# Two chained expert layers after sigmoid attention: block sums split where they are made, tokens loaded into free slots, stores on GpSimd's queue

## The chip, the cores and the metric

One core of a Trainium2 chip. The metric is the device time of one execution, in microseconds. A core has TensorE (PE; its weight loads are PEld), VectorE (DVE), ScalarE (ACT), GpSimd (POOL), SyncE (SP), and 16 DMA engines that serve all queues. Each engine runs its instructions in the order in which they were written.

## What is computed

```python
scores = scale * np.matmul(q, k.transpose(0, 1, 3, 2)) - np.log(S)   # q, k, v: 4 x 12 x 448 x 64
attn = 1.0 / (1.0 + np.exp(-scores))
x = np.matmul(attn, v)                         # then heads side by side: x is 1792 x 768
h = x @ w_in;  g = s * np.maximum(h, 0.0) ** 2 + b;  x = g @ w_out        # w_in 768 x 2048, w_out 2048 x 768
h = x @ w_in2; g = np.maximum(h, 0.0) + alpha * np.minimum(h, 0.0); out = g @ w_out2
```

All arrays are float32.

## The kernel before

**Arithmetic.** Each of the four large products is one step of a seven-product block scheme: the weights are cut in 2 x 2 blocks, sums of blocks (A11, A12, A22, S1 to S4) are made, and so are sums of token blocks; products M1 to M7 are formed in `IN_ORDER` or `OUT_ORDER` (lines 23 and 24) and added up on eviction. Each float32 operand is split in a rounded part (L322, ScalarE) and the rest (L325, VectorE), and each product is three matmuls, L406 to L408, of a 128 x 128 weight tile with 448 tokens.

**Stages.** First attention, in `NU` = 84 units (`qk`, `sig`, `av`, `take_x`). Then the tokens go through in two halves g = 0, 1, for each expert layer m = 0, 1: `phases` are (m, g) = (0,0), (0,1), (1,0), (1,1), and each has an in-phase (8 groups `mp` of seven products with the non-linear function after them) and an out-phase (seven products, three output blocks each). So eight half-phases of 504 matmuls follow attention.

**Weights.** The weights come in as 64-bit words. `quad` (L236) makes one block sum's worth: two loads into `R64`, `cva` on ScalarE (L263), L266 and L271 on VectorE, four additions (L284), and a store of 7 blocks to a DRAM tile (L302). There are 8 of kind "in" and 9 of kind "out" for each m, all made in the one buffer `QUAD`. `unit` (L309) loads 1024 columns of that DRAM tile into `RAW` and splits them into a `RING` entry, 21 units for every half-phase.

**Tokens.** `make_x` makes the seven token operands `X` out of four raw blocks `XRAW`, with VectorE subtractions (L335) and splits. For phases after the first, `load_x` loads the raw blocks from DRAM to `XRAW[1]`, which lies in `PROD`, over `R64`, `CVA` and a part of `QUAD`. It and `make_x` are written at the last product of the out-phase before (`middle[6]`).

**PSUM.** In an in-phase products M1 and M2 use one bank, M5 and M4 another, M6 and M7 a third: the second of each accumulates on the first, and must wait until the first was read (`pcopy` L417, `padd` L427).

**Order.** Everything but warm-up is added to a `Plan` with an engine, a cost and the cells that it reads and writes. `order` (L55) sets due times from TensorE's order and then, over and over, emits for the engine that can start first the operation that can start first, by those costs. The `"SP"` queue is one such engine, and carries all loads and all stores (L302, L526). Block sums are asked for by `produce`: 20 at attention unit 4, 9 after phase 0, the rest after phase 1.

Of the kernel before, what the change touches and what calls it, by code (L numbers as in the profile page):

```python
# [18 lines left out]
CELL = 64  # L19

IN_ORDER = ["M1", "M5", "M6", "M2", "M7", "M4", "M3"]
# [5 lines left out]
class Plan:  # L29
# [25 lines left out]
    def order(self):  # L55
# [5 lines left out]
        ideal, t = {}, 0.0  # L61
        for i, op in enumerate(self.ops):
            if op[0] == "PE":
                ideal[i] = t
                t += op[1]
        late = [0.0] * n
        for i in range(n - 1, -1, -1):
            eng, dur, lat = self.ops[i][:3]
            x = min((late[s] for s in succ[i]), default=t + 50) - dur - lat
            late[i] = min(x, ideal[i]) if i in ideal else x  # L70
        left = [len(op[3]) for op in self.ops]
        est = [0.0] * n
        pe = [i for i in range(n) if i in ideal]
# [5 lines left out]
        free = {}  # L79
        done = []  # L80
        while len(done) < n:
            best = None
            for eng, cand in open_.items():
                if not cand:
                    continue
                f = free.get(eng, 0.0)
                if eng == "PE":
# [13 lines left out]
            end = start + dur  # L101
            free[eng] = end
            done.append(i)
            for s in succ[i]:
                est[s] = max(est[s], end + lat)
# [3 lines left out]
        return done  # L109
# [26 lines left out]
def tile_kernel(  # L136
# [59 lines left out]
    RAW = [own(f"raw{i}", UNIT) for i in range(NRAW)]  # L196
    TMP = [own(f"tmp{i}", S) for i in range(NTMP)]
    NEG = own("neg", 2 * S)
# [7 lines left out]
    def act_t(n, psum=False):  # L206
        return (0.15 if psum else 0.19) + 0.834e-3 * n

    def dve_t(n, psum=False):
        return 0.155 + (1.06e-3 if psum else 1.04e-3) * n  # L210
# [4 lines left out]
    def dma_t(n):  # L215
        return 0.1 + n * 4 * P / 330e3
# [3 lines left out]
    MM = 0.2005  # L220
# [11 lines left out]

    w64 = {(0, "in"): w_in1, (0, "out"): w_out1, (1, "in"): w_in2, (1, "out"): w_out2}
    w32 = {k: drp.tile([P, 7 * NMP * WQ], F32, name=f"w{k[0]}{k[1]}") for k in w64}

    def quad(m, kind, k, c):  # L236

        order = IN_ORDER if kind == "in" else OUT_ORDER
# [8 lines left out]
        for row in range(2):  # L247
# [9 lines left out]
            x, y = ("A11", "A12") if row == 0 else ("S3", "A22")  # L257
# [18 lines left out]
            add("ACT", act_t(2 * n), f0, cv, ca)  # L276
# [11 lines left out]
        tt("S1", "S3", "A22", ALU.add)  # L288
        tt("S3", "A11", "S3", ALU.subtract)
# [7 lines left out]
        else:  # L297
# [4 lines left out]
            "SP", dma_t(7 * n), lambda: nc.sync.dma_start(out=dst, in_=src),  # L302
# [3 lines left out]
    n_unit = [0]  # L306
    ring = {}

    def unit(m, kind, i):  # L309
        g = n_unit[0]  # L310
        n_unit[0] += 1
        raw, dst = RAW[g % NRAW], RING[g % NRING]
        load(
            sb(raw, UNIT), w32[m, kind][:, i * UNIT : (i + 1) * UNIT], UNIT,
            [("d", m, kind, 8 * i + j) for j in range(8)], cells(raw, UNIT),
        )
        split(dst, dst + UNIT, raw, UNIT)
        ring[m, kind, i] = dst
# [27 lines left out]
    X = [[slots(f"xo{p}{i}", p, 3 * i, 3) for i in range(7)] for p in range(2)]  # L346
# [17 lines left out]
    def make_x(par, raw):  # L364
        p = [XRAW[raw] + i * XB for i in range(4)]
        pl = X[par]

        def half(i, src):
            split(pl[i], pl[i] + XB, src, XB)

        half(0, p[0])
        minus(p[0], p[1], p[0], XB)
        half(1, p[0])
        minus(p[0], p[3], p[0], XB)
        half(2, p[0])
        half(3, p[2])
        minus(p[1], p[3], p[1], XB)
        half(4, p[1])
        minus(p[0], p[0], p[2], XB)
        half(5, p[0])  # L380
        half(6, p[3])

    def load_x(m, g):
        for i in (0, 1, 3, 2):
            to = XRAW[1] + i * XB
            load(
                sb(to, XB), x_dram[m, g][:, i * XB : (i + 1) * XB], XB,
# [458 lines left out]
```

## Time and profile before

| | us |
|---|---|
| median of 3 runs | 1026.64 (1022.49 to 1033.18) |
| profiled execution | 1022.74 |
| its span, first to last instruction | 1020.9 |
| TensorE busy in the span | 972.0 (95%) |
| VectorE busy | 762.6 (75%) |
| ScalarE busy | 625.8 (61%) |
| GpSimd busy | 0.2 |
| moved by DMA | 222.7 MB, 218 GB/s on the mean |

A row of a group of instructions names line, engine, operation and tiles (out<-in). PEclk is the granted share of TensorE's clock. TensorE's busy time is that of pipelined matmuls, so a busy TensorE can still be waiting a little.

### The profile page before, as it was taken

What the parts mean: (1) busy time and instruction counts of PE and PEld (TensorE: products, weight loads), DVE (VectorE), ACT (ScalarE), POOL (GpSimd) and SP (SyncE); (2) the same over time, 40 slices, a digit from 0 to 9 for tenths busy, and PEclk for the clock granted to TensorE, in tenths of its full rate; (3) what the DMA queues carried; (4) which work ended last, traced back from release to release, by engine and by line L of the source; (5) the groups of instructions that cost most, each with busy time, mean ns of one, the idle gap of its engine ahead of it and who ended that gap; (6) DMA issues with size and microseconds to landing.
All of it is one profiled execution on the core that took longest, in us unless ns stands there. A gap on an engine that the chain in (4) does not pass through costs nothing.

```text
span 1020.9 us, 13856 instructions
## 1 busy us (share of the span) xinstructions
PE 972.0 (95%) x5424; PEld 828.7 (81%) x5424; DVE 762.6 (75%) x896; ACT 625.8 (61%) x675; POOL 0.2 (0%) x4
## 2 busy tenths in 40 slices
PE   9999999998699979999999889998999999999998
PEld 5533368987598968999899769997999999999997
DVE  2476467679996867668999589868997856679872
ACT  7889856877553536778665246656645455576440
POOL 0000000000000000000000000000000000000000
PEclk9999999998899999999999989998999999999999
DMA  8998999886776657776579568765444533333441
GB/s 302 332 336 300 354 330 353 281 286 193 275 258 223 208 185 285 239 253 222 166 241 313 198 233 281 226 216 200 116 122 147 163 111 111 104 106 105 146 138 67
DMA packets 70625, 222.68 MB, mean 218 GB/s; under 512 B 6688, under 2 KB 30624, under 8 KB 68512
## 3 DMA queue, kind: packets, MB, share of 16 engines
q1 hardware_dynamic: 70560, 221.81, 64.6%
q8 instruction: 42, 0.69, 0.3%
q14 instruction: 23, 0.19, 0.0%
HBM read 163.98 MB, written 57.80 MB: 217 GB/s over the span
## 4 chain that ended last, share of the span: by engine, by line
PE 62%; DVE 11%; DMA 6%; ACT 3%; issue 3%; SPq 0%; DVEq 0%; ACTq 0%
PE ps L406 21%; PE ps L408 21%; PE ps L407 21%; DMA xraw<-x 3%; DVE ring L325 2%; DVE xo L325 2%; DVE gb L325 1%; DVE g L335 1%; DVE quad L284 1%; DMA r<-in_w_in 1%; DVE xraw L335 1%; DVE tmp L427 1%; ACT gb L322 1%; DVE quad L271 1%; DMA raw<-w0in 1%
## 5 line engine op out<-in xcount | busy, mean ns | idle before, releaser
L406 PE MATMUL ps<-xo,ring 128*128 128x448 f32 x672 | 250.9, 373 | 22.3 <-DVE tmp L427 18.7
L322 ACT CAST ring<-raw 128x1024 fp32r<-128x1024 f32 x168 | 175.3, 1047 | 154.6 <-PE ps L407 111.9
L406 PE MATMUL ps<-gb,ring 128*128 128x448 f32 x672 | 249.1, 371 | 10.7 <-ACT ring L322 7.5
L408 PE MATMUL ps<-gb,ring 128*128 128x448 f32 x672 | 249.0, 371 | 9.4 <-DVE ring L325 9.4
L407 PE MATMUL ps<-xo,ring 128*128 128x448 f32 x672 | 249.0, 370 | 0.0
L408 PE MATMUL ps<-xo,ring 128*128 128x448 f32 x672 | 248.7, 370 | 0.0
L407 PE MATMUL ps<-gb,ring 128*128 128x448 f32 x672 | 248.1, 369 | 0.0
L325 DVE TENSOR_TENSOR ring<-raw,ring 128x1024 fp32r<-128x1024 f32 x168 | 204.2, 1217 | 24.7 <-ACT ring L322 24.6
L406 PEld LDWEIGHTS ps<-xo,ring 128*128 128x128 f32 x672 | 128.6, 191 | 39.3 <-DVE tmp L427 23.1
L406 PEld LDWEIGHTS ps<-gb,ring 128*128 128x128 f32 x672 | 128.2, 191 | 23.4 <-ACT ring L322 10.6
L408 PEld LDWEIGHTS ps<-gb,ring 128*128 128x128 f32 x672 | 128.0, 190 | 22.1 <-DVE ring L325 11.5
L408 PEld LDWEIGHTS ps<-xo,ring 128*128 128x128 f32 x672 | 128.5, 191 | 10.7
L407 PEld LDWEIGHTS ps<-xo,ring 128*128 128x128 f32 x672 | 128.5, 191 | 10.3
L407 PEld LDWEIGHTS ps<-gb,ring 128*128 128x128 f32 x672 | 128.3, 191 | 10.4
L427 DVE TENSOR_TENSOR tmp<-ps,tmp 128x448 f32<-128x448 f32 x124 | 76.7, 619 | 71.0 <-PE ps L408 58.2
L325 DVE TENSOR_TENSOR gb<-g,gb 128x1344 fp32r<-128x1344 f32 (+1 forms) x84 | 116.1, 1395 | 10.1 <-ACT gb L322 7.7
L322 ACT CAST gb<-g 128x1344 fp32r<-128x1344 f32 (+1 forms) x84 | 99.3, 1190 | 21.2 <-PE ps L408 14.5
L677 ACT ACTIVATE sg<-ps,bias 128x896 f32<-128x896 f32 x84 | 82.9, 1009 | 13.3 <-PE ps L661 12.6
L263 ACT ACTIVATE cva<-r 128x768 f32<-128x768 f32 (+1 forms) x68 | 59.0, 868 | 51.5 <-DVE quad L271 20.0
L271 DVE SCALAR_TENSOR_TENSOR quad<-cva,quad 128x768 uint32<-128x768 uint32 (+1 forms) x68 | 61.5, 905 | 30.6 <-DMA xraw<-x 18.5
L661 PE MATMUL ps<-kq 64*64 64x448 f32 x672 | 80.9, 542 | 2.0 <-ACT sg L677 2.0
L699 PE MATMUL ps<-sg,v 64*64 64x448 f32 x672 | 80.0, 536 | 0.0
(32 smaller groups left out, 656.8 us busy)
## 6 DMA issues: line engine op xcount, KB each, us to landing
r<-in_w_in SPq DMA_DIRECT2D x32, 768.0 KB, 5.4
raw<-w0in SPq DMA_DIRECT2D x42, 512.0 KB, 4.5
raw<-w0out SPq DMA_DIRECT2D x42, 512.0 KB, 4.3
raw<-w1in SPq DMA_DIRECT2D x42, 512.0 KB, 3.7
raw<-w1out SPq DMA_DIRECT2D x42, 512.0 KB, 3.5
r<-in_w_out SPq DMA_DIRECT2D x24, 768.0 KB, 5.9
w0in<-quad SPq DMA_DIRECT2D x8, 1344.0 KB, 7.5
w1in<-quad SPq DMA_DIRECT2D x8, 1344.0 KB, 5.3
```

Source lines behind the costliest of these rows:

```text
L263: nc.scalar.activation(a, hi, AF.Prelu, scale=2.0**-112, alpha=-(2.0**32))
L271: nc.vector.scalar_tensor_tensor(out=u, in0=a.bitcast(U32), scalar=3, in1=u, op0=ALU.logical_shift_left, op1=ALU.bitwise_or,)
L322: add("ACT", act_t(n), lambda: nc.scalar.copy(h, x), cells(src, n), cells(hi, n))
L325: lambda: nc.vector.tensor_tensor(out=l, in0=x, in1=h.bitcast(F32), op=ALU.subtract),
L335: lambda: nc.vector.tensor_tensor(out=o_, in0=x_, in1=y_, op=ALU.subtract),
L406: nc.tensor.matmul(d, wh_, ml_, start=first and k == 0, stop=False, **opt)
L407: nc.tensor.matmul(d, wh_, mh_, start=False, stop=False, **opt)
L408: nc.tensor.matmul(d, wl_, mh_, start=False, stop=last and k == n, **opt)
L427: lambda: nc.vector.tensor_tensor(out=d, in0=bank(k), in1=o, op=ALU.add),
L661: nc.tensor.matmul(ps[h * D : (h + 1) * D, k + j, :S], a.ap[rows, S + k0 : S + k0 + D], a.ap[rows, :S], start=True, stop=True,)
L677: lambda: nc.scalar.activation(o, i, AF.Sigmoid, bias=sb(BIAS, 1), scale=QKSCALE),
L699: nc.tensor.matmul(ps[j * D : (j + 1) * D, k + h, :S], va[keys, v : v + D], a.ap[keys, j * S : (j + 1) * S], start=first, stop=last,)
```

## The change

Block sums for the first in-phase are kept in on-chip memory and split from there (`direct`), with a second buffer (`quadb`) over the place of `RAW` and `NEG`; they are still stored for the second half. Two in-sums and seven out-sums are asked for in attention, the other six in-sums and two out-sums inside the first in-phase, and all of m = 1 after that phase. Raw tokens (`XRAW[1]`) lie in five slots between the others, and in `NEG`. `IN_ORDER` has M4 before M7. All stores are issued by GpSimd. The plan is placed three times, each time with TensorE's start times of the time before as goals; loads and stores share one modelled pipe there, and some costs are changed. `MORE` is empty, so nothing is saved in split form.

```diff
-IN_ORDER = ["M1", "M5", "M6", "M2", "M7", "M4", "M3"]
+QUEUES = {"SP": 0.07, "POOL": 1.0}
+AHEAD = 1.0
+ROUNDS = 3
+EARLY = 7
+MORE = []
+IN_ORDER = ["M1", "M5", "M6", "M2", "M4", "M7", "M3"]
...
+        for _ in range(ROUNDS):
+            late = [0.0] * n
+            for i in range(n - 1, -1, -1):
+                dur, lat = self.ops[i][1:3]
+                x = min((late[s] for s in succ[i]), default=t + 50) - dur - lat
+                late[i] = min(x, goal[i]) if i in goal else x
+            done, at = self.place(succ, late, list(goal))
+            goal = {i: at[i] for i in goal}
+        return done
...
                 f = free.get(eng, 0.0)
+                if eng in QUEUES:
+                    f = max(f, pipe - AHEAD)
...
-            end = start + dur
-            free[eng] = end
+            if eng in QUEUES:
+                free[eng] = start + QUEUES[eng]
+                pipe = max(pipe, start) + dur
+                end = pipe
+            else:
+                end = free[eng] = start + dur
...
-    XRAW = {0: tensor("xraw0", RING0, 4 * XB), 1: tensor("xraw1", PROD, 4 * XB)}
+    SPARE = take(NRAW * UNIT + 2 * S)
+    RING4 = [tensor(f"rinq{i}", RING0 + i * 4 * WQ, 4 * WQ, F32R) for i in range(4)]
+    RAW = [tensor(f"raw{i}", SPARE + i * UNIT, UNIT) for i in range(NRAW)]
+    NEG = tensor("neg", SPARE + NRAW * UNIT, 2 * S)
+    MID = SLOTS + 16 * SLOT
+    XRAW[1] = [
+        [(tensor("xraw10", MID + 2 * SLOT, XB), 0, XB)],
+        [(tensor("xraw11", MID, XB), 0, XB)],
+        [(tensor("xraw12", MID + 2 * SLOT + XB, XB), 0, XB)],
+        [(tensor("xraw13", MID + XB, S), 0, S), (tensor("xraw14", NEG.base, 2 * S), S, XB)],
+    ]
-    QUAD = tensor("quad", PROD + 10 * WQ, 7 * WQ)
+    QUADS = [tensor("quad", PROD + 10 * WQ, 7 * WQ), tensor("quadb", SPARE, 7 * WQ)]
...
-    MM = 0.2005
+    MM = 0.2035
...
-        tt("S1", "S3", "A22", ALU.add)
-        tt("S3", "A11", "S3", ALU.subtract)
+        tt("S3", "A11", "S1", ALU.subtract)
+        tt("S1", "S1", "A22", ALU.add)
...
-            "SP", dma_t(7 * n), lambda: nc.sync.dma_start(out=dst, in_=src),
+            "POOL", dma_t(7 * n), lambda: nc.gpsimd.dma_start(out=dst, in_=src),
...
+    def direct(mp, place):
+        for b0, b1 in ((0, 2), (2, 4), (4, 6), (6, 7)):
+            n = (b1 - b0) * WQ
+            dst = entry((7 * mp + b0) * WQ, n, RING4)
+            split(dst, dst + n, QUADS[place] + b0 * WQ, n)
+            yield
...
-    X = [[slots(f"xo{p}{i}", p, 3 * i, 3) for i in range(7)] for p in range(2)]
+    X = [
+        [slots(f"xo{p}{i}", 0, k, 3) for i, k in enumerate(ks)]
+        for p, ks in enumerate(([0, 3, 6, 9, 12, 18, 15], [34, 31, 28, 25, 22, 19, 16]))
+    ]
...
+            if m == g == 0:
+                get = direct(mp, 1 - mp % 2)
             for i, x in enumerate(IN_ORDER):
...
+                    if m == g == 0 and i % 2 == 0 and kc == 0:
+                        next(get)
...
+            if m == 0 and g == 0 and mp + 2 < NMP:
+                if mp % 2 == 1 and EARLY + mp // 2 < len(outs):
+                    quad(*outs[EARLY + mp // 2])
+                quad(m, "in", mp + 2, 0, 1 - mp % 2)
...
-        add("SP", dma_t(S), lambda: nc.sync.dma_start(out=d, in_=x), cells(src, S), w, DMA_LAT)
+        add("POOL", dma_t(S), lambda: nc.gpsimd.dma_start(out=d, in_=x), cells(src, S), w, DMA_LAT)
...
-    for m in range(2):
-        quads += [(m, "in", k, 0) for k in range(NMP)]
-        quads += [(m, "out", k, c) for c in range(len(CHUNKS)) for k in range(NDP)]
+    quads = [(0, "in", 0, 0, 1)]
+    outs = [(0, "out", k, c) for c in range(len(CHUNKS)) for k in range(NDP)]
+    quads += outs[:EARLY]
+    quads += [(0, "in", 1, 0, 0)]
+    quads += [(1, "in", k, 0) for k in range(NMP)]
+    quads += [(1, "out", k, c) for c in range(len(CHUNKS)) for k in range(NDP)]
...
-            produce(20)
+            produce(2 + EARLY)
...
+        if n == 0:
+            produce(len(quads))
         middle = {}
...
-        if n == 0:
-            produce(9)
-        if n == 1:
-            produce(len(quads))
```

## Rows read from the trace of the kernel before

**Rows 1.** Busy time by stretch (start:end, length; xinstructions; PEclk, DMA share, GB/s).

```profile
0.00:134.00 134.00, 130.96 (x1392) 61.24 (x1392) 71.09 (x101) 115.02 (x134) 0.20 (x4) 1.00 0.90 323
134.00:248.00 114.00, 105.72 (x508) 95.53 (x504) 85.60 (x125) 80.95 (x82) 0.00 (x0) 0.98 0.86 296
248.00:369.40 121.40, 110.17 (x505) 98.56 (x506) 102.66 (x110) 61.35 (x66) 0.00 (x0) 0.93 0.67 226
369.40:481.70 112.30, 104.75 (x505) 95.61 (x504) 79.06 (x107) 77.71 (x75) 0.00 (x0) 0.98 0.74 254
481.70:591.70 110.00, 104.51 (x505) 95.71 (x505) 95.00 (x102) 59.25 (x63) 0.00 (x0) 0.98 0.69 227
591.70:710.20 118.50, 108.87 (x506) 98.46 (x505) 97.81 (x129) 70.02 (x84) 0.00 (x0) 0.94 0.70 236
710.20:812.40 102.20, 102.20 (x506) 94.64 (x506) 90.30 (x80) 56.89 (x57) 0.00 (x0) 1.00 0.43 131
812.40:915.10 102.70, 102.50 (x505) 94.50 (x504) 66.07 (x77) 58.21 (x69) 0.00 (x0) 1.00 0.36 108
915.10:1017.40 102.30, 102.30 (x505) 94.50 (x504) 74.35 (x69) 46.35 (x48) 0.00 (x0) 1.00 0.38 118
```

The five busy times in a row are PE, PEld, DVE, ACT and POOL.

**Rows 2.** Waits of PE: who for whom, us in total, times, longest.

```profile
PE ps L406 <- DVE tmp L427: 20.0, 10, 5.0
PE ps L408 <- DVE ring L325: 9.4, 5, 3.6
```

**Rows 3.** Chain that ended last, 310 to 345 us: start, us, what.

```profile
311.76 5.35 DMA xraw<-x
...
326.84 5.14 DMA w1in<-quad
...
332.00 3.87 DMA xraw<-x
```

**Rows 4.** Tile `quad`: ns min/median/max, first to last start; then idle causes.

```profile
L302 SPq DMA_DIRECT2D w0out<-quad x9: 525/525/604, 148.4 to 262.0; - x9
...
L302 SPq DMA_DIRECT2D w0in<-quad x8: 326/326/424, 27.4 to 132.4; - x8
...
  DMA xraw<-x: 24.8, 6
```

**Rows 5.** DMA issues: count, KB each, median us to landing.

```profile
raw<-w0in SPq DMA_DIRECT2D x42, 512.0 KB, 4.5
...
w0in<-quad SPq DMA_DIRECT2D x8, 1344.0 KB, 7.5
w1in<-quad SPq DMA_DIRECT2D x8, 1344.0 KB, 5.3
...
out_yt<-tmp SPq DMA_DIRECT2D x24, 224.0 KB, 1.9
...
sc<-in_s SPq DMA_DIRECT2D x1, 0.5 KB, 6.5
```

**Rows 6.** Groups of instructions by form: busy, mean ns, idle before.

```profile
L325 DVE TENSOR_TENSOR ring<-raw,ring 128x1024 fp32r<-128x1024 f32 x168 | 204.2, 1217 | 24.7 <-ACT ring L322 24.6
...
L427 DVE TENSOR_TENSOR tmp<-ps,tmp 128x448 f32<-128x448 f32 x124 | 76.7, 619 | 71.0 <-PE ps L408 58.2 <-ACT tmp L417 10.4 <-PE ps L661 1.8
...
L284 DVE TENSOR_TENSOR quad<-quad 128x384 f32<-128x384 f32 x112 | 57.7, 551 | 5.8 <-DMA xraw<-x 4.0 <-ACT xo L322 0.9
L271 DVE SCALAR_TENSOR_TENSOR quad<-cva,quad 128x768 uint32<-128x768 uint32 x56 | 53.3, 952 | 24.6 <-DMA xraw<-x 14.5 <-ACT cva L263 10.1
...
L266 DVE TENSOR_SCALAR quad<-r 128x768 uint32<-128x768 uint32 x56 | 29.1, 554 | 25.0 <-DMA w0in<-quad 14.5 <-DMA w0out<-quad 5.2 <-DMA r<-in_w_in 5.2
```

**Rows 7.** Busy time by stretch, one of 25 us in the third out-phase.

```profile
725.00:750.00 25.00, 25.00 (x125) 23.16 (x125) 25.00 (x22) 12.11 (x13) 0.00 (x0) 1.00 0.44 129
```

**Rows 8.** Waits of SyncE's queue: who for whom, us in total, times, longest.

```profile
SPq L229 <- DVE ring L325: 450.5, 150, 7.9
SPq L302 <- DVE quad L284: 55.3, 26, 4.3
```

More of the change, by code (lines that the diff above doesn't have):

```diff
@@ L60, in order, with place @@
                 succ[d].append(i)
-        ideal, t = {}, 0.0
+        goal, t = {}, 0.0
         for i, op in enumerate(self.ops):
             if op[0] == "PE":
-                ideal[i] = t
+                goal[i] = t
                 t += op[1]
[L66 to L70, printed above, removed]
+        for _ in range(ROUNDS):
[7 more added lines that the diff above has]
+        return done
+    def place(self, succ, late, pe):
+        n = len(self.ops)
         left = [len(op[3]) for op in self.ops]
         est = [0.0] * n
-        pe = [i for i in range(n) if i in ideal]
         pe_at = 0
@@ L78, in order @@
                 open_.setdefault(self.ops[i][0], set()).add(i)
-        free = {}
-        done = []
+        free, done, at = {}, [], {}
+        pipe = 0.0
         while len(done) < n:
@@ L301, in quad, with saved, entry, unit @@
         add(
-            "SP", dma_t(7 * n), lambda: nc.sync.dma_start(out=dst, in_=src),
+            "POOL", dma_t(7 * n), lambda: nc.gpsimd.dma_start(out=dst, in_=src),
             cells(QUAD, 7 * n), wrote, DMA_LAT,
         )
-    n_unit = [0]
+    whl = {k: drp.tile([P, 2 * 7 * NMP * WQ], F32R, name=f"s{k[0]}{k[1]}") for k in SAVED}
+    n_unit = [0, 0]
     ring = {}
-    def unit(m, kind, i):
-        g = n_unit[0]
+    def saved(m, kind, at, n):
+        return whl[m, kind][:, 2 * at : 2 * (at + n)], [("h", m, kind, at)]
+    def entry(at, n, ring_=RING):
+        dst = ring_[n_unit[0] % len(ring_)]
         n_unit[0] += 1
-        raw, dst = RAW[g % NRAW], RING[g % NRING]
+        for j in range(n // P):
+            ring[at // P + j] = (dst + j * P, dst + (n + j * P))
+        return dst
+    def unit(m, kind, i, g):
+        at, n = i * UNIT, UNIT
+        dst = entry(at, n)
+        if (m, kind) in SAVED and g == 1:
+            src, there = saved(m, kind, at, n)
+            load(sb(dst, 2 * n), src, 2 * n, there, cells(dst, 2 * n))
+            return
+        raw = RAW[n_unit[1] % NRAW]
+        n_unit[1] += 1
         load(
-            sb(raw, UNIT), w32[m, kind][:, i * UNIT : (i + 1) * UNIT], UNIT,
-            [("d", m, kind, 8 * i + j) for j in range(8)], cells(raw, UNIT),
-        )
-        split(dst, dst + UNIT, raw, UNIT)
-        ring[m, kind, i] = dst
+            sb(raw, n), w32[m, kind][:, at : at + n], n,
+            [("d", m, kind, 8 * i + j) for j in range(8)], cells(raw, n),
+        )
+        split(dst, dst + n, raw, n)
+        save(m, kind, at, n, dst)
+    def save(m, kind, at, n, dst):
+        if (m, kind) in SAVED:
+            d, there = saved(m, kind, at, n)
+            x = sb(dst, 2 * n)
+            add(
+                "SP", dma_t(2 * n), lambda: nc.sync.dma_start(out=d, in_=x),
+                cells(dst, 2 * n), there, DMA_LAT,
+            )
+    def direct(mp, place):
[4 more added lines that the diff above has]
+            yield
     def split(hi, lo, src, n):
@@ L364, in make_x, with less @@
     def make_x(par, raw):
-        p = [XRAW[raw] + i * XB for i in range(4)]
-        pl = X[par]
+        p, pl = XRAW[raw], X[par]
         def half(i, src):
-            split(pl[i], pl[i] + XB, src, XB)
+            for t, a, e in src:
+                split(pl[i] + a, pl[i] + (XB + a), t, e - a)
+        def less(o, x, y):
+            for t, a, e in x if len(x) > 1 else y:
+                n = e - a
+                o_, x_, y_ = (z[0][0] + a if len(z) == 1 else t for z in (o, x, y))
+                minus(o_, x_, y_, n)
         half(0, p[0])
-        minus(p[0], p[1], p[0], XB)
+        less(p[0], p[1], p[0])
         half(1, p[0])
-        minus(p[0], p[3], p[0], XB)
+        less(p[0], p[3], p[0])
         half(2, p[0])
         half(3, p[2])
[L377 to L380, printed above, removed]
+        less(p[0], p[0], p[2])
+        half(4, p[0])
+        less(p[1], p[3], p[1])
+        half(5, p[1])
         half(6, p[3])
@@ L704, in f @@
                 )
[L706 removed]
+        add("PE", 0.80, f, r + w, w, PE_LAT)
     def take_x(q):
@@ L712, in take_x @@
         o = (2 * kh + bb % 2) * XB + i * S
-        t = XRAW[0] + o if bb < 2 else tmp()
+        t = XRAW[0][2 * kh + bb][0][0] + i * S if bb < 2 else tmp()
         pcopy(t, k)
```

64 lines of the change are left out of this document (31 added, 33 removed).

## The prediction

> **What bounds the kernel now.** I read the time by stretches first, cut where TensorE changes its work [rows 1]: attention (0 to 134 us), then four in-phases and four out-phases of 504 matmuls each. The last three take 102.2, 102.7 and 102.3 us, and TensorE is busy for all but 0.2 us of them: that is the floor of a half-phase, TensorE-bound at a granted clock of 1.00. The five before them take 114.0, 121.4, 112.3, 110.0 and 118.5 us, 576.2 together, which is 64 us above five floors of 102.45 (the mean of the 102.2 and the 102.7). The clock in those five rows is 0.93 to 0.98, so part of the excess is matmuls run slower after a stall. Attention has DMA busy 0.90 of the time at 323 GB/s and ScalarE busy 115 of 134 us.
>
> What ends TensorE's waits [rows 2]: the first matmul of a group waits for `tmp` from L427 (20.0 us, 10 times), that is a VectorE eviction of a PSUM bank that the next product accumulates in; and half of a ring entry comes late from L325 (9.4 us). These rows name the last link. The chain of waits names the cause behind it. At 310 to 336 us [rows 3], the end of the first out-phase, it alternates between the tokens' loads (`xraw<-x`, 5.35 and 3.87 us among them) and a block sum's store (`w1in<-quad`, 5.14 us): XRAW[1] lies in PROD, over R64, CVA and QUAD, so the next tokens land where a block sum is still being made, and each waits for the other. VectorE's block-sum instructions alone sat idle 24.8 us for `xraw<-x` [rows 4]. The first out-phase's beginning has another cause: 17 block sums of `m` = 0 are made one after another in one buffer, at (132.4 - 27.4)/7 = 15.0 and then (262.0 - 148.4)/8 = 14.2 us each [rows 4], so the last store leaves at 262.0 us, 14 us into the phase that reads it.
>
> **The change, part by part.** *Attention.* Nine block sums are asked for instead of a free run of 20; before, eight were stored by 132.4 us [rows 4]. Loads, stores and ScalarE's 115 us stay about as they are, TensorE's rate too. I take 0, from -3 (fewer ScalarE instructions between sigmoids) to +3.
>
> *First in-phase.* 21 of the 42 `raw<-w0in` loads of 512 KB go [rows 5], 11 MB. The splits now read QUADS directly, so block sum mp+2 is made while product group mp runs. VectorE decides. One group of seven products costs it 2688 columns of splits at 1.217 us per 1024 (3.2 us, some 3.4 in four instructions), five PSUM additions at 0.619 (3.1), and, for one block sum, 2 x 0.554 + 2 x 0.952 + 4 x 0.551 = 5.2 us [rows 6]: 11.7 us, in a group of 102.45/8 = 12.8. Eight groups of splits and additions are 52 us, six and a half block sums 34, the two out-sums left over (one is two thirds wide) 9: 95 us. The highest share that VectorE has in a phase at the floor is 90.3 of 102.2, 0.884 [rows 1]; 95/0.884 = 107.5. So the phase lies between 102.45 and 107.5 if nothing else stalls, and above that if a sum comes late. I take 108, against 114: -6. The order M2, M4, M7 helps here: M7, which accumulates in M6's bank, came two products after M6 and now comes three, M4 after M5 three instead of four. One product is three terms of three matmuls, 12.7/7 = 1.8 us, which is about the mean wait on L427 (20.0/10 = 2.0 us [rows 2]).
>
> *First out-phase to third in-phase.* XRAW[1] moves into five slots that are free in an out-phase, and NEG; the tokens' loads then wait for no block sum, and no sum for them. All 17 sums of `m` = 0 are finished by then, and the 17 of `m` = 1 have the stretch to about 650 us. At 14.2 us each [rows 4] they need 241 us of the 412 there are, so their pace is no bound. VectorE's work is unchanged: 102.7 + 79.1 + 95.0 + 97.8 = 374.5 us [rows 1]. At the floor these four phases take 409.8; if VectorE can't go above 0.884, 374.5/0.884 = 423.7. I take 419, two thirds of the way, since it does reach 25.0 of 25 us with TensorE at 25.0 in some stretches [rows 7]. Before: 121.4 + 112.3 + 110.0 + 118.5 = 462.2. So -43.
>
> *The last three phases* are at their floor: 0.
>
> *Stores on GpSimd's queue.* SyncE's queue stood 55.3 us before stores until their sums were done [rows 8], with loads behind. That queue is freed, but what mostly holds the loads is their own buffer (450.5 us for `ring`), so I count nothing for it. GpSimd does nothing in this trace but four memsets, and no row shows what a DMA from its queue costs. Call the delay of a store's landing L. Its bounds: below, -1 us or so, a store that no longer waits behind loads; above, 6.5 us, what even 0.5 KB took to land in a full queue [rows 5]. I take 1 us: the nearest row is the smallest store on an idle queue, `out_yt<-tmp`, 1.9 us of which 224 KB at 323 GB/s are 0.7, so 1.2 fixed, and a second such fixed part is the guess. Where L hurts: seven sums of attention stand in line for QUADS[0], so (0, "in", 1) comes 7L later. By the pace of 15.0 us (the first, in the other buffer, out at 27.4, the second 8 later) the seventh leaves near 35 + 6 x 15 = 125, lands near 132 and the in-sum is ready near 139; its splits start near 134 + 12.8 - 2 = 144.6. That is 5 us of slack. Two more out-sums stand before in-sums 3 and 5, with 1 and 3 us of slack. The price is 9L - 9 us: 0 at L = 1. The end gets 1 us longer by L (the last store ends the span).
>
> *A rule against it.* L266 takes 554 ns for 768 columns, L271 952 [rows 6], so L266 runs at about double rate and the other sum instructions don't. The Trainium skill (SBUF — State Buffer, Summary: rules for kernel authors) says of just such instructions that they lock GpSimd out while it writes a DMA's descriptors, and advises SyncE's or ScalarE's queue instead. By that rule a store waits for up to one L266, L grows by 0.55, and the sum by 5 us. No row here shows it, since GpSimd issues nothing.
>
> **Sum.** The profiled execution took 1022.74 us (span 1020.9). 1022.74 - 6 - 43 + 1 = 974.7, say 975. It lies 0.4% under the median of 1026.64, so the forecast stands a little low against that.
>
> **Rivals.** *Stores land late on GpSimd's queue (L = 3).* For: the seven stores in line are the only long serial chain that the change makes. Against: 15 us of pace has slack in it. 9 x 3 - 9 = 18: 993.
>
> *VectorE becomes the bound.* It needs 374.5 of 409.8 us. Where it was mixed with sums it reached 95.0 of 110.0 and 97.8 of 118.5, 0.84 on the mean [rows 1]; 374.5/0.84 = 446, 27 more than I count: 1002. Against: 24.8 us of its idle time is waits of the sums for `xraw<-x` [rows 4], which go.
>
> *The handovers stay.* What holds them could be the splits of the tokens (11 instructions of 1344 columns on VectorE, by the 1.217 us for 1024 [rows 6] an estimated 1.6 each, 17 us) and not their loads; then out-to-in handovers keep their excess in the second and third in-phases, 112.3 + 118.5 - 2 x 102.45 = 26, and some 9 of the out-phases before: 1010. Against: the fourth handover does the same splits with the tokens loaded before, and its phase is at the floor [rows 1].
>
> *Slower.* One mechanism: the line of stores through QUADS[0] in attention and the first in-phase, with GpSimd's landing so late that TensorE starves in the first in-phase. It decides from 9L - 9 = 48, L = 6.3 us, a landing of 12 to 14 us where 5.3 to 7.5 were [rows 5]. At L = 8: 63 us, 1038. For: the out-sums' stores are cut in seven rows per partition, and GpSimd's price is unknown. Against: even 6.5 us took a full queue.
>
> **How the numbers follow.** Forecast 975 (its own range 960 to 988): 0.56. Late stores 993: 0.16. VectorE 1002: 0.12. Handovers stay 1010: 0.08. Slower 1038: 0.08. A change of 1% is about what can be told from none here (three runs lie 1022.5 to 1033.2). Faster by over 1% (below 1016): the first three and a quarter of the fourth, 0.86; within 1%: the rest of the fourth, 0.06; slower 0.08. The range runs from 958 (attention 3 us shorter, phases near 410 and 103) to 1005; the last two cases lie above it, and some of the first three at its ends.
>
> **What would show it.** First out-phase to third in-phase each 103 to 107 us with clock 0.98 or more; no `xraw<-x` in the chain; waits on `tmp` L427 under 6 us; no store of `w0out` after 200 us; first in-phase near 108. Wrong, if the wait before the first in-phase's ring splits is for a store or a block sum (late stores), if VectorE is above 0.9 of those phases and TensorE still waits for L325, or if GpSimd's issues show several us each.

## The result and the profile after

The changed kernel takes 996.5 us (median of 4 runs, 992.3 to 1004.0) against 1024.9 for the kernel before: 0.9717 of it, 95% interval 0.9635 to 0.9799. The forecast was 975 with a range of 958 to 1005. The time lies in the range, and the gain is 28 us where 48 were summed. The profiled execution took 992.3 us, its span is 990.1.

Busy time of the changed kernel by stretch, cut where TensorE changes its work, with the columns of [rows 1] (PE, PEld, DVE, ACT, POOL; then PEclk, DMA share, GB/s); the last row is the end after the last matmul:

```profile
0.00:138.30 138.30, 133.15 (x1393) 61.24 (x1393) 73.03 (x104) 115.55 (x138) 13.26 (x23) 1.00 0.89 318
138.30:241.80 103.50, 102.39 (x508) 94.55 (x504) 93.16 (x147) 78.66 (x87) 6.13 (x10) 1.00 0.74 267
241.80:346.40 104.60, 102.80 (x505) 94.61 (x506) 96.71 (x94) 66.20 (x69) 7.32 (x13) 1.00 0.61 205
346.40:448.50 102.10, 102.10 (x505) 94.62 (x504) 77.46 (x103) 75.70 (x74) 3.22 (x6) 1.00 0.75 260
448.50:550.70 102.20, 102.20 (x506) 94.69 (x506) 95.78 (x93) 62.13 (x64) 6.50 (x12) 1.00 0.56 187
550.70:652.90 102.20, 102.20 (x506) 94.48 (x504) 91.31 (x127) 65.34 (x78) 6.82 (x8) 1.00 0.84 291
652.90:778.00 125.10, 108.36 (x506) 97.44 (x506) 105.11 (x104) 63.26 (x66) 7.76 (x13) 0.93 0.49 158
778.00:880.10 102.10, 102.10 (x505) 94.65 (x504) 66.05 (x78) 57.73 (x69) 0.54 (x1) 1.00 0.37 110
880.10:984.50 104.40, 104.23 (x505) 94.36 (x504) 75.41 (x70) 46.31 (x48) 5.96 (x11) 1.00 0.37 115
984.50:990.10 5.60, 0.00 (x0) 0.00 (x0) 0.62 (x1) 0.00 (x0) 0.54 (x1) 0.86 0.10 41
```

| us | before | by the prediction's sum | after |
|---|---|---|---|
| attention | 134.0 | 134.0 | 138.3 |
| first in-phase | 114.0 | 108 | 103.5 |
| first out-phase to third in-phase | 462.2 | 419 | 411.1 |
| third out-phase | 102.2 | 102.2 | 125.1 |
| last two phases | 205.0 | 205.0 | 206.5 |
| end | 3.5 | 4.5 | 5.6 |
| span | 1020.9 | 972.7 | 990.1 |

What was to be gained was gained, 12 us more than summed in the first five phases. But a phase that was at its floor before has a new stall of 23 us. TensorE's waits (who for whom, us in total, times, longest), to be read beside [rows 2]:

```profile
PE ps L480 <- ACT ring L386: 11.0, 3, 6.1
PE ps L480 <- DVE gb L389: 4.7, 3, 2.7
PE ps L482 <- DVE ring L389: 4.0, 4, 1.7
```

TensorE's waits on `tmp` are gone from the half-phases, and waits on a ring's split (11.0 and 4.0 us) hold most of what is left. Behind the longest of them, on the chain that ended last between 640 and 690 us (start, us, what), and then in the timeline of SyncE, ScalarE and TensorE (start, us; in brackets the engine's idle time before and what ended it):

```profile
659.42 5.59 DMA w1out<-quad
```

```profile
665.06 6.45 SPq L257 DMA_DIRECT2D raw<-w1out  x2
...
668.45 1.04 ACT L386 CAST ring<-raw 128x1024 fp32r<-128x1024 f32 x1 [1.44 <-DMA raw<-w1out]
...
669.55 0.74 PE L480 MATMUL ps<-gb,ring 128*128 128x448 f32 x1 [6.09 <-ACT ring L386]
```

TensorE waits for a weight whose block sum is stored only now: the load leaves as the store lands (659.42 + 5.59 = 665.01), the split follows the load, and the matmul the split. This store leaves 6.5 us into the phase that reads it, the last one 17 us. Not all of the 23 us is standing: TensorE's busy time in that phase is 108.4 instead of 102.2, so some 6 us are matmuls that ran slower. After TensorE had stood, the granted clock was about 0.5, the lower of its two levels (1.2 of 2.4 GHz):

```profile
665.00:675.00 10.00, 4.90 (x13) 3.94 (x14) 9.79 (x14) 4.22 (x6) 0.89 (x1) 0.52 0.51 157
```

The stores of the sums, by name (tile `quad`: ns min/median/max, first to last start), beside [rows 4]:

```profile
L332 POOL DMA_DIRECT2D w0out<-quad x9: 891/902/939, 35.0 to 187.5; - x9
L332 POOL DMA_DIRECT2D w1out<-quad x9: 891/895/912, 557.9 to 670.3; - x9
L332 POOL DMA_DIRECT2D w1in<-quad x8: 533/539/539, 297.0 to 541.2; - x8
```

The out-sums of m = 0 now end at 187.5 us, 54 us before the phase that reads them (before: 262.0, 14 us inside it). The eight in-sums of m = 1 take from 297 to 541 us, far more than eight times 14 us. The nine out-sums leave from 557.9 to 670.3, one each 14.1 us, and the last two of them in the third out-phase.

### The profile page after: what moved, and what is told of

The parts are those of the page before. It is cut to its first block, busy times and chain, and to the rows that moved or that the text cites. A ratio compares the mean times of both kernels' runs of the same rounds, so it can differ in the third digit from the quotient of the medians.

```text
span 990.1 us, 13931 instructions
## 1 busy us (share of the span) xinstructions
PE 959.5 (97%) x5424; PEld 820.7 (83%) x5424; DVE 774.6 (78%) x916; ACT 630.9 (64%) x689; POOL 58.1 (6%) x98
## 4 chain that ended last, share of the span: by engine, by line
PE 49%; issue 41%; DMA 3%; DVE 2%; POOL 2%; ACT 2%; POOLq 0%; SPq 0%; ACTq 0%; DVEq 0%
PE ps L482 13%; PE ps L480 13%; PE ps L481 13%; PE ps L740 5%; PE ps L778 4%; DMA r<-in_w_out 1%; DMA r<-in_w_in 1%; ACT sg L756 1%; POOL x L606 1%; POOL w1out L332 1%; POOL out_yt L606 1%; DMA w1out<-quad 1%; DVE ring L389 0%; ACT cva L293 0%; DVE g L399 0%
## 5 line engine op out<-in xcount | busy, mean ns | idle before, releaser
L386 ACT CAST ring<-raw 128x1024 fp32r<-128x1024 f32 x147 | 153.8, 1047 | 142.4 <-PE ps L481 123.9
L389 DVE TENSOR_TENSOR ring<-raw,ring 128x1024 fp32r<-128x1024 f32 x147 | 179.3, 1220 | 27.1 <-ACT ring L386 26.7
L480 PE MATMUL ps<-xo,ring 128*128 128x448 f32 x504 | 184.1, 365 | 0.0
L481 PE MATMUL ps<-xo,ring 128*128 128x448 f32 x504 | 184.1, 365 | 0.0
L482 PE MATMUL ps<-xo,ring 128*128 128x448 f32 x504 | 184.1, 365 | 0.0
L481 PEld LDWEIGHTS ps<-gb,ring 128*128 128x128 f32 x672 | 127.4, 190 | 10.5
L480 PEld LDWEIGHTS ps<-xo,ring 128*128 128x128 f32 x504 | 94.7, 188 | 7.5
L482 PEld LDWEIGHTS ps<-xo,ring 128*128 128x128 f32 x504 | 94.7, 188 | 7.5
L481 PEld LDWEIGHTS ps<-xo,ring 128*128 128x128 f32 x504 | 94.7, 188 | 7.5
L740 PE MATMUL ps<-kq 64*64 64x448 f32 x672 | 86.7, 545 | 2.9 <-ACT sg L756 2.7
L778 PE MATMUL ps<-sg,v 64*64 64x448 f32 x672 | 86.6, 536 | 1.2 <-DVE tmp L501 1.2
L399 DVE TENSOR_TENSOR g<-g 128x1344 f32<-128x1344 f32 (+1 forms) x48 | 66.3, 1396 | 2.3 <-ACT xo L386 2.2
```

The costliest lines, as they stand in the source:

```text
L386: add("ACT", act_t(n), lambda: nc.scalar.copy(h, x), cells(src, n), cells(hi, n))
L389: lambda: nc.vector.tensor_tensor(out=l, in0=x, in1=h.bitcast(F32), op=ALU.subtract),
L399: lambda: nc.vector.tensor_tensor(out=o_, in0=x_, in1=y_, op=ALU.subtract),
L480: nc.tensor.matmul(d, wh_, ml_, start=first and k == 0, stop=False, **opt)
L481: nc.tensor.matmul(d, wh_, mh_, start=False, stop=False, **opt)
L482: nc.tensor.matmul(d, wl_, mh_, start=False, stop=last and k == n, **opt)
```

## The experiments

### Is the new stall the late sums, and what makes them late?

Three theories. A: VectorE has no more time for the sums. B: stores from GpSimd land later, and that stretches the cycle of each sum. C: the plan's due times. It is placed three times, and each time takes TensorE's delayed starts as the new goals, so a late sum no longer counts as late.

**The sums of the second out-weight left out.**

```diff
-            sb(raw, n), w32[m, kind][:, at : at + n], n,
-            [("d", m, kind, 8 * i + j) for j in range(8)], cells(raw, n),
+            sb(raw, n), w32[0 if kind == "out" else m, kind][:, at : at + n], n,
+            [("d", 0 if kind == "out" else m, kind, 8 * i + j) for j in range(8)], cells(raw, n),
...
-    quads += [(1, "out", k, c) for c in range(len(CHUNKS)) for k in range(NDP)]
```

> The changed kernel without the nine out-sums of m = 1: the last two out-phases read the out-sums of m = 0 instead, so the second layer's second weight is left out. Theory A or any theory in which these sums are the cause of the new stall: third out-phase from 125.1 to 102 to 104 us, everything before the third in-phase unchanged to 1 us, profiled time about 992.3 - 22 = 970, which is close to the 975 that was forecast. A rival, that the stall comes from the tokens' loads into the middle slots and NEG (xraw loads at 651 to 674 us, with landings of 6.5 to 8.4 us) or from the handover itself: the third out-phase keeps at least 10 us of its excess.

The time of one run was 980.3 us, the span 978.6. The third out-phase, same columns as above:

```profile
664.40:767.00 102.60, 102.46 (x506) 94.57 (x505) 92.56 (x85) 57.15 (x59) 5.97 (x11) 1.00 0.50 159
```

125.1 to 102.6: the stall goes with the sums, shown. Tokens and handover are still there, so by themselves they have no part in it beyond 0.4 us. The time fell by 12 and not by 22 us, since attention took 3 us more here, the first out-phase 106.8 instead of 104.6, and the three phases after it 104.2 instead of 102.1 to 102.2 (see the last section).

**Stores on SyncE's queue, the plan told so.**

```diff
-            "POOL", dma_t(7 * n), lambda: nc.gpsimd.dma_start(out=dst, in_=src),
+            "SP", dma_t(7 * n), lambda: nc.sync.dma_start(out=dst, in_=src),
...
-        add("POOL", dma_t(S), lambda: nc.gpsimd.dma_start(out=d, in_=x), cells(src, S), w, DMA_LAT)
+        add("SP", dma_t(S), lambda: nc.sync.dma_start(out=d, in_=x), cells(src, S), w, DMA_LAT)
```

> The changed kernel with all stores issued by SyncE again, nothing else. Theory A (the third out-phase stalls because the block sums of m = 1 get too little of VectorE before it): the stall stays, third out-phase 120 to 127 us against 125.1, and the time lies within 5 us of the changed kernel's 992 to 997. Theory B (the store's landing from GpSimd's queue, 6.2 us median against 5.8 before, lengthens the cycle of a sum, and 17 sums in one buffer add that up): landing falls by about 1 us, nine sums of the third in-phase end some 9 us earlier, third out-phase about 112 us, time about 982. For attention (138.3 against 134.0 us before): if GpSimd's queue is its cause, it returns to 134; if the nine sums asked for there are, it stays at 138. The end after the last matmul should return from 5.6 to 3.5 us in either case.

993.2 us (984.5 to 997.7), 0.965 of before (0.9589 to 0.9711). The third out-phase took 123.9 us, where B asked for about 112: B falls. (With SyncE's stores in the changed kernel's own order it is 125.8, below.) Attention, from the first matmul, took 135.6, the end 3.4.

**One placing of the plan.**

```diff
-ROUNDS = 3
+ROUNDS = 1
```

> The changed kernel, its plan placed once and not three times, so due times are those of a TensorE that never waits. Theory C (each further round takes TensorE's delay of the round before as its goal, so the late sums of m = 1 no longer count as late, and stay behind work that isn't urgent): sums start earlier in the second out-phase or third in-phase, third out-phase 106 to 112 us, third in-phase up to 110, sum of the two 218 to 220 against 227.3, time about 8 us less than the changed kernel's. Theory A in its strict form (VectorE simply has no more time there): no gain, the stall only moves to the third in-phase. Theory B: no gain either, since the cycle of a sum is what it was.

983.4 us (980.7 to 984.3 in three runs; a fourth took 997.3), 0.9557 of before (0.9499 to 0.9614). Third in-phase and third out-phase:

```profile
553.40:660.10 106.70, 102.89 (x505) 94.39 (x504) 96.93 (x139) 68.07 (x83) 8.26 (x10) 1.00 0.81 284
660.10:771.00 110.90, 106.24 (x505) 96.66 (x505) 98.28 (x90) 58.69 (x60) 6.85 (x12) 0.97 0.50 161
```

217.6 together against 227.3, as C said. In the third in-phase VectorE spent 37.3 us on the sums instead of 34.2, the phase grew by 4.5 us, and the last `w1out` store left at 660.5 instead of 670.3; over the two phases VectorE stood idle 22.4 us instead of 30.9.

**One placing, and the sums of m = 1 due 15 us earlier.**

```diff
-ROUNDS = 3
+ROUNDS = 1
+HURRY = 15
...
+            for i in self.early:
+                late[i] -= HURRY
...
+            if m == 1:
+                plan.early.update(range(first, len(plan.ops)))
```

> As the one-round kernel, and all block sums of m = 1 are due 15 us earlier than the plan says. Theory C: a little more than one round alone, about 12 us less than the changed kernel (984 of 996 in medians), third in-phase and third out-phase together about 214 us against 227.3. Theory A in its strict form: VectorE's busy share from 242 to 778 us (466 of 536 us in the changed kernel) can't rise, the sum of the phases from the first out-phase to the third stays at 536. Theory B: no change above 3 us.

980.2 us (972.3 to 985.2), 0.9527 of before (0.9468 to 0.9586); the two phases took 108.2 and 104.4, together 212.6, and the last `w1out` store left at 651.9 us instead of 670.3. So the plan's due times are shown as the cause of 15 of the 22 us that the two phases had over the floor: 10 by the repeated placing, which is C, and 5 more by the earlier due times. A holds for what is left at most: in the third in-phase VectorE was busy 99.4 of 108.2 us.

### What does the queue cost?

**The kernel before with its stores on GpSimd, the plan told.**

```diff
-            "SP", dma_t(7 * n), lambda: nc.sync.dma_start(out=dst, in_=src),
+            "POOL", dma_t(7 * n), lambda: nc.gpsimd.dma_start(out=dst, in_=src),
```

(and the same in `store`)

> The kernel before with one part of the change: all stores issued by GpSimd. What the prediction held: loads no longer stand behind stores, but mostly wait for their own buffers, and a landing is 1 us later, so within 1% of before, 1017 to 1033. If the queue of SyncE was what delayed the loads, 10 us or more faster. If late landings hurt the chain of 17 sums in one buffer (15 us each up to 262 us), each sum takes 1 us longer and the first out-phase begins 10 to 17 us later: 1033 to 1040. In any case the end after the last matmul grows from 3.5 to about 5.6 us.

1044.8 us (1037.7 to 1048.1), 1.0148 of before (1.0098 to 1.0197). Attention, from the first matmul, grew from 133.0 to 143.8 us, but this plan holds GpSimd's stores for a second pipe, so its order differs too. The next run takes that away.

**The kernel before, its own order, only the issuing engine changed.**

```diff
-            "SP", dma_t(7 * n), lambda: nc.sync.dma_start(out=dst, in_=src),
+            "SP", dma_t(7 * n), lambda: nc.gpsimd.dma_start(out=dst, in_=src),
```

(and the same in `store`)

> The kernel before with every instruction in the order of the kernel before, the stores issued by GpSimd instead of SyncE; the plan isn't told. The run in which the plan was told took 1.0148 of before (1.0098 to 1.0197), attention 143.8 us against 133.0. If GpSimd's landing (6.16 us median for the sums against 5.81) is what cost that, this one is 1 to 2% slower too, attention about 140. If it was the plan, which took GpSimd's stores for a second pipe beside the loads and so put sums' instructions on ScalarE and VectorE too early, this one is within 0.5% of before, with attention at 131 to 134 and only the end 2 us longer.

1040.0 us (1038.1 to 1041.2), 1.0128 of before (1.0093 to 1.0162). The expectation was half right: the queue costs by itself, but not in attention (134.8 from 133.0). The cost is 6 us in the first out-phase (127.5), 5.5 in the second (115.5), 2.4 in the first in-phase and 3 at the end; the second in-phase took 2.7 less. The stores of the chained sums of m = 0, beside [rows 4]:

```profile
L302 POOL DMA_DIRECT2D w0out<-quad x9: 891/895/900, 150.7 to 267.7; - x9
...
L302 POOL DMA_DIRECT2D w0in<-quad x8: 531/531/671, 26.8 to 134.6; - x8
```

The last leaves 5.7 us later than the 262.0 of before, and the first out-phase ends 10.4 us later (at 379.8 instead of 369.4). So the later chain of sums can carry about half of that delay; that it does is not shown, and what adds the rest stays open.

**The changed kernel, its own order, stores issued by SyncE.**

```diff
-            "POOL", dma_t(7 * n), lambda: nc.gpsimd.dma_start(out=dst, in_=src),
+            "POOL", dma_t(7 * n), lambda: nc.sync.dma_start(out=dst, in_=src),
```

(and the same in `store`)

> The changed kernel with every instruction in its order, the stores issued by SyncE; the plan isn't told, so a load may stand behind a store that waits. If GpSimd's queue costs time by itself: attention 2 to 4 us shorter than 137 to 140, the end 2 us shorter, 0.963 to 0.967 of before as in the run whose plan was told. If SyncE's queue blocks loads: TensorE waits for raw loads again and the time is above the changed kernel's 0.9717.

991.1 us (986.0 to 994.3), 0.9649 of before (0.9599 to 0.9698). The intervals of this and of the changed kernel (0.9635 to 0.9799) overlap, so the queue's cost in the changed kernel isn't settled by the times; the end is 2.2 us shorter, third out-phase and end being

```profile
652.30:778.10 125.80, 110.25 (x506) 99.20 (x505) 104.39 (x102) 62.45 (x66) 0.00 (x0) 0.92 0.47 157
...
982.90:986.30 3.40, 0.01 (x1) 0.00 (x0) 0.62 (x1) 0.00 (x0) 0.00 (x0) 0.90 0.18 67
```

No phase is longer by more than 0.7 us for the loads that now stand behind stores. The landing of stores from GpSimd, in the changed kernel (issues: KB each, median us to landing):

```profile
w1in<-quad POOLq DMA_DIRECT2D x8, 1344.0 KB, 5.4
...
w0out<-quad POOLq DMA_DIRECT2D x6, 1344.0 KB, 8.7
...
out_yt<-tmp POOLq DMA_DIRECT2D x24, 224.0 KB, 2.2
```

and of the same stores from SyncE, in this one:

```profile
w1in<-quad SPq DMA_DIRECT2D x8, 1344.0 KB, 5.0
w0out<-quad SPq DMA_DIRECT2D x6, 1344.0 KB, 8.1
...
out_yt<-tmp SPq DMA_DIRECT2D x24, 224.0 KB, 1.9
```

0.3 to 0.6 us more; over all nine kinds of store the medians differ by -0.1 to 1.2 us. The last store adds how long the issue comes after VectorE's last instruction (timeline: start, us; the idle time of that engine in brackets), first from GpSimd, then from SyncE:

```profile
984.50 0.62 DVE L501 TENSOR_TENSOR tmp<-ps,tmp 128x448 f32<-128x448 f32 x1 [4.33 <-PE ps L482]
985.42 0.54 POOL L606 DMA_DIRECT2D out_yt<-tmp  x1 [4.42 <-DVE tmp L501]
```

```profile
982.95 0.62 DVE L501 TENSOR_TENSOR tmp<-ps,tmp 128x448 f32<-128x448 f32 x1 [4.24 <-PE ps L482]
983.60 0.33 SPq L606 DMA_DIRECT2D out_yt<-tmp  x1
```

0.30 us (985.42 - 985.12) against 0.03, in this one store. So by these rows a store is some 0.6 to 0.9 us later from GpSimd.

### Which part brought the gain?

**The kernel before with the raw tokens in the free slots.**

```diff
-    XRAW = {0: tensor("xraw0", RING0, 4 * XB), 1: tensor("xraw1", PROD, 4 * XB)}
+    XRAW[1] = [
+        [(tensor("xraw10", MID + 2 * SLOT, XB), 0, XB)],
+        [(tensor("xraw11", MID, XB), 0, XB)],
+        [(tensor("xraw12", MID + 2 * SLOT + XB, XB), 0, XB)],
+        [(tensor("xraw13", MID + XB, S), 0, S), (tensor("xraw14", NEG.base, 2 * S), S, XB)],
+    ]
...
```

> The kernel before with one part of the change: the raw tokens of later phases in the five middle slots and NEG instead of over the buffers of the block sums; the old product order is kept. The prediction's step: the wait of sums and tokens for each other goes, so the second and third in-phases lose most of their excess (112.3 and 118.5 towards 103 to 106) and the two out-phases before them part of it; 20 to 30 us faster, about 1000. Rival (the handovers are held by VectorE's splits of the tokens): under 10 us faster, and these phases stay above 110.

1000.8 us (999.9 to 1002.4), 0.9744 of before (0.9718 to 0.977), nearly the gain of the whole change. First out-phase to third in-phase:

```profile
250.20:370.30 120.10, 111.12 (x504) 98.91 (x505) 108.33 (x120) 64.65 (x66) 0.00 (x0) 0.94 0.75 258
370.30:474.50 104.20, 104.20 (x506) 94.66 (x505) 78.08 (x108) 75.13 (x72) 0.00 (x0) 1.00 0.78 264
474.50:579.30 104.80, 102.43 (x505) 94.63 (x504) 99.34 (x100) 63.49 (x67) 0.00 (x0) 1.00 0.63 205
579.30:686.70 107.40, 105.36 (x505) 95.73 (x505) 84.25 (x117) 64.05 (x78) 0.00 (x0) 0.98 0.66 218
```

The last three lose most of their excess (the third in-phase keeps 5 us); the first out-phase keeps 120, where the sums of m = 0 still come in a chain (the last `w0out` store at 261.7 us), and the first in-phase took 118.5 us instead of 114.1. So the parts work at different places: the tokens' move on the second and third in-phases and the out-phase between them, the other parts (sums split in place and asked for earlier) on the first in-phase and the first out-phase, which took 104.2 and 104.9 us with the tokens back in their old place, in the next run.

**The changed kernel with the tokens back over the sums' buffers, the sums in three lots.**

```diff
-    XRAW[1] = [
-        [(tensor("xraw10", MID + 2 * SLOT, XB), 0, XB)],
...
+    XRAW[1] = [[(tensor(f"xraw1{i}", PROD + i * XB, XB), 0, XB)] for i in range(4)]
...
-            produce(len(quads))
+            produce(3)
...
+        if n == 0:
+            produce(9)
+        if n == 1:
+            produce(len(quads))
```

> The changed kernel with the raw tokens of later phases back over the buffers of the block sums, and the sums of m = 1 asked for in three lots as before (3, 9, 5), since a lot must end before the next tokens come. If the tokens' place is what keeps the handovers short (their move alone took the kernel before to 0.974), the second and third in-phases or the out-phases before them lose 8 us or more each again, third out-phase about 104, time 1000 to 1015. The plan's own account says otherwise: no loss at the handovers, 113 us for the third in-phase, 103.5 for the third out-phase, in all some 10 us less than the changed kernel; then the handovers' excess in the kernel before came from sums that ran late against the plan, not from the place as such.

985.4 us (984.2 to 990.5), 0.9593 of before (0.9555 to 0.9631): faster than the changed kernel (0.9635 to 0.9799), if barely, not slower. The first out-phase to the second took 104.9, 103.5 and 102.1 us. One handover still shows the collision, between 548 and 572 us (waits):

```profile
PE ps L475 <- DVE xo L384: 12.6, 2, 11.8
ACT xo L381 <- DMA xraw<-x: 9.1, 2, 6.8
```

The third in-phase took 117.9 us by that. In return a lot of sums must be done before the next tokens may land, which can hurry them as a due time would: the last `w1out` store left at 661.0, 10 us before the third out-phase, which took 104.2 us. So the shared place alone isn't what made the handovers of before long, as two of three went with next to no stall. That it takes late sums beside it fits this and was not tried by itself.

**The product order alone**, on the kernel before (M2, M4, M7, and the sums and token sums put in the order that it needs).

```diff
-IN_ORDER = ["M1", "M5", "M6", "M2", "M7", "M4", "M3"]
+IN_ORDER = ["M1", "M5", "M6", "M2", "M4", "M7", "M3"]
...
-        tt("S1", "S3", "A22", ALU.add)
-        tt("S3", "A11", "S3", ALU.subtract)
+        tt("S3", "A11", "S1", ALU.subtract)
+        tt("S1", "S1", "A22", ALU.add)
...
```

> The kernel before with one part of the change: product order M2, M4, M7 and the block sums renamed so that it can be (S1 made in the place of the sum of row 1). If the short distance from M6 to M7 is what makes TensorE wait for tmp of L427 (20.0 us, 10 waits), those waits fall below 8 us and the in-phases are 5 to 12 us shorter in total. If the eviction is late because VectorE stands for tokens or sums, the waits stay above 14 us and the time within 1%.

1025.5 us in one run, no gain beyond the spread of before. The waits on `tmp` did fall, from 20.0 us [rows 2]:

```profile
PE ps L406 <- ACT ring L322: 26.1, 4, 13.5
PE ps L406 <- DVE tmp L427: 6.5, 3, 3.3
```

but those on the ring's first split grew to 26.1 from 7.5, in the kernel before

```profile
PE ps L406 <- ACT ring L322: 7.5, 4, 3.5
```

and the first in-phase grew from 114.1 to 122.2 us. A wait that is taken away where something else is late a little further on only changes its name.

**The old order in the changed kernel.**

```diff
-IN_ORDER = ["M1", "M5", "M6", "M2", "M4", "M7", "M3"]
+IN_ORDER = ["M1", "M5", "M6", "M2", "M7", "M4", "M3"]
...
```

> The changed kernel with the old product order M2, M7, M4 and the rest of the change kept. If the order is worth something by itself, the in-phases (103.5, 102.1, 102.2, 102.1 us) grow by 1 to 4 us each, with waits on the eviction of M6. If VectorE is simply no longer late, they stay at 102 to 104, and the third out-phase moves by what the plan makes of the sums.

989.2 us in one run. The in-phases took 105.7, 102.2, 108.0 and 102.1 us: the first and third grow by 2 and 6, the others don't. The third out-phase fell to 117.7, so the plan only moved the sums' stall. No gain of the new order shows in the time: this one run lies below all four of the changed kernel (992.3 to 1004.0).

### The best of it

One placing, the sums of m = 1 due 15 us earlier, and all stores on SyncE's queue, the plan told so.

```diff
-ROUNDS = 3
+ROUNDS = 1
+HURRY = 15
...
+            for i in self.early:
+                late[i] -= HURRY
...
-            "POOL", dma_t(7 * n), lambda: nc.gpsimd.dma_start(out=dst, in_=src),
+            "SP", dma_t(7 * n), lambda: nc.sync.dma_start(out=dst, in_=src),
...
```

> The changed kernel with one placing, the sums of m = 1 due 15 us earlier, and all stores issued by SyncE. If the two gains add (hurry: 0.9527 against 0.9717; SyncE: 0.965 against 0.9717) the ratio to before is about 0.946, some 970 us; end after the last matmul 3.4 us. If SyncE's gain in its first run was only spread, 0.952.

970.0 us (969.5 to 974.3), 0.9456 of before (0.9419 to 0.9493), which beats both kernels. Third in-phase and third out-phase:

```profile
549.20:655.80 106.60, 103.67 (x506) 94.25 (x505) 100.31 (x139) 69.05 (x84) 0.00 (x0) 1.00 0.80 274
655.80:760.60 104.80, 104.05 (x506) 94.54 (x505) 94.69 (x87) 57.19 (x60) 0.00 (x0) 1.00 0.47 159
```

## Why the prediction was right, and where it wasn't

That the time lies in the stated range is in part luck. It lies outside the forecast's own range, 960 to 988, and inside the stated one, 958 to 1005, because that was widened for rivals, and their mechanisms did not act. The steps that were to gain gained 12 us more than summed, and a stall that the sum did not have, with attention, took 27.

**First out-phase to third in-phase, -43: right, and more (-51).** The four phases took 411.1 us, near the lower bound of 409.8. VectorE was busy 361.3 us of them, 0.879, about the 0.884 that was taken for its highest share. But that was possible because two sums were put off to the phase after: where all were stored by the end of the third in-phase, the four took 415.6 us (the best kernel) and 422.7 (one placing, due earlier), about the 419 of the sum. The mechanism (tokens and sums wait for each other over one place) was there: moving the tokens alone gave 0.9744. The signs named for it came too: no `xraw<-x` on the chain that ended last, the last `w0out` store at 187.5 us, no wait of a half-phase on `tmp`. It was told too simply, though: with the tokens in the old place and the sums in three lots, two of three handovers cost next to nothing.

**First in-phase, -6: right, and more (-10.5).** VectorE's 95 us were 93.2. The assumption that it can't go above 0.884 was too cautious: 93.16 of 103.5 is 0.90, and 100.31 of 106.6 in the best kernel's third in-phase 0.94.

**The last three phases, "at their floor: 0": wrong, +23.** This is the step that failed, and with it the sentence that 17 sums at 14.2 us each need 241 us of the 412 there are, "so their pace is no bound". The pace was right where sums ran one behind the other (14.1 us each from 557.9 to 670.3). What was wrong is that they could run at that pace all the time. In the two out-phases VectorE is busy 96.7 and 95.8 of 104.6 and 102.2 us, only 9.0 and 7.1 of it with sums, and the plan gives a sum what splits, differences and tokens leave: two sums were stored in the first out-phase, one in the second. That leaves the sums some 204 us in two in-phases, about half the 412; at 14.2 us each these hold 14, so with the three just the 17, and no slack. It was used up in the second in-phase: five sums were stored there, 20.6 us apart (357.1 to 439.6), although VectorE stood idle for 24.6 of its 102.1 us. What held them there no run tried; with one placing they came no faster (20.7 us). So the nine out-sums, which the phase from 652.9 reads, left only from 557.9 to 670.3. The sum of VectorE's work over the stretch hid in which phases it is free. [rows 1] had a sign of it: the third out-phase, which has no sums in it, left VectorE 11.9 us free of 102.2, and one sum takes 5.2 of VectorE alone.

**Attention, 0: +4.3, its cause open.** From its first matmul, nine kernels with the changed attention took 135.2 to 140.4 us for it, three of them with stores on SyncE (135.6, 136.6, 135.6), against 130.7 to 134.8 for four with that of before (a fifth, the one whose plan was told of GpSimd's stores, took 143.8). Six of the nine run it with the same instructions in the same order on each engine, and it is these six that lie from 135.2 to 140.4: one order spreads over 5 us by itself, as much as the 4.3 in question. The queue isn't the main part: where only the issuing engine was changed, it made 0.6 us (137.2 against 136.6) and, in the kernel before, 1.8. That leaves what the plan puts into attention; it wasn't tried.

**Stores, L = 1 us, price 0: size about right.** A store is 0.6 to 0.9 us later by the rows above, and the end grew by 2.1 instead of 1 us. The kernel before, whose 17 sums of m = 0 stand in one chain, lost 1.3% by the queue alone, for which the chain accounts in part at most; that this part of the change is a loss by itself the prediction had not said, as the price formula was written only for the sums of the changed kernel. In the changed kernel no loss is shown. By its own terms the price at L = 1 was 2 us and not 0: 7L is 2 us over the first slack of 5, and what is left over of a later slack doesn't pay for that. The first in-phase, at 103.5 us, shows neither. The 55.3 us that SyncE's queue stood before stores were those for sums only; before the stores of L526 it stood another 104 us. That nothing was counted for its freeing was right even so: with the order kept, moving the stores off it made the kernel before slower.

**The rule against it.** The instruction in question took, in the changed kernel (busy, mean ns):

```profile
L296 DVE TENSOR_SCALAR quad<-r 128x768 uint32<-128x768 uint32 x48 | 26.7, 556 | 20.0 <-DMA w0out<-quad 13.3 <-DMA w1out<-quad 3.3 <-DMA w1in<-quad 1.9
```

556 ns against 554 [rows 6], so VectorE isn't held up. GpSimd is, but seldom: only two of its 94 issues overlap with one of the 68 instructions of this line. One overlaps by 0.05 us and took no longer; the other spans one whole (timeline: start, us) and is the longest of 36 issues of its kind, whose median is 542 ns:

```profile
342.88 0.83 POOL L606 DMA_DIRECT2D x<-tmp  x1 [3.12 <-DVE tmp L509]
...
343.04 0.55 DVE L296 TENSOR_SCALAR quad<-r 128x768 uint32<-128x768 uint32 x1
```

It ended 0.12 us after that instruction. The kernel before with GpSimd's stores in its own order has one such issue too, of 827 ns where the median is 543. The Trainium skill (SBUF — State Buffer, Summary: rules for kernel authors) advises against GpSimd's queue because such an instruction starves it; these two issues agree. But it's 0.29 us once, and the 1.3% that the kernel before lost did not come by that road. The prediction's 0.55 us for each store was too much, since the two seldom meet. The Trainium skill (DMA: Bandwidth & Descriptors, Specifications) gives about 1 us to the first byte on GpSimd's path and 0.6 on SyncE's, 0.4 more; the 0.3 to 0.6 us of landing above agree.

**The rivals.** Late stores: no, the stall stays with SyncE's stores (123.9 and 125.8 us). VectorE as the bound: not in the form told (411 us, not 446), but in the out-phases it is what leaves the sums little room. Handovers stay: no. Slower: no.

## What to carry to other kernels

An engine's total over a long stretch says nothing of when it is free; work that fills gaps must be counted against the gaps ahead of its due time, phase by phase. A scheduler that takes its own delayed times as goals forgets what is late; one placing with earlier due times gave 15 us back here. Split a change that has a queue in it: on the kernel before, the move of the stores was a loss of 1.3% on its own, beside parts that gained. And run one order several times before a few us of one stage are explained: attention spread over 5.

## What the hardware showed that was not expected

TensorE ran the same stream at one of two paces with no wait between. The last in-phase, 778.0 to 880.1 us in the profile above, took 102.1 us; in the best kernel, with as many matmuls and TensorE busy throughout at the same granted clock,

```profile
760.60:864.80 104.20, 104.20 (x506) 94.65 (x505) 66.37 (x79) 57.77 (x70) 0.00 (x0) 1.00 0.34 108
```

That is 202.7 or 206.7 ns from one matmul's start to the next. In the traces the pace mostly changes at a stall and then holds to the next, through whole half-phases: in the kernel without the second out-sums four phases in a row took 104.2 us or more. Twice it changed with no wait beside it: in the kernel before at 212 us, and in that kernel with GpSimd's stores in its own order at 727 us. It is 2 us for each half-phase and may be a part of the spread between runs of one kernel; what chooses the pace was not tried.

After the last store was issued by GpSimd the program still ran 4.7 us (985.42 to 990.1), from SyncE 2.7 (983.60 to 986.3), though the landing differs by 0.3.
